# Bias of seven opening M units through TensorE, an earlier third table and later weight loads in a spectral layer with an ELU feed-forward, Trainium2

## The chip, the core and the metric

The kernel runs on one core of a Trainium2 chip. The metric is the time of one execution on the device in microseconds (us). Five engines work side by side, each through its own queue in order: TensorE (PE, matmuls; PEld its weight loads), VectorE (DVE), ScalarE (ACT), GpSimd (POOL) and SyncE (SP), which here only issues transfers. POOL issues transfers too. Matmul results lie in PSUM, everything else in SBUF; DA, DB, inputs and output lie in device memory.

## The reference

Eight sequences of 3008 tokens with 256 features go through a complex linear layer in the frequency domain, a soft threshold, the way back, and then a feed-forward layer with an ELU:

```python
X = np.fft.rfft(x, axis=1)
Yr = Xr @ w_r - Xi @ w_i + b_r
Yi = Xr @ w_i + Xi @ w_r + b_i
Yr = np.sign(Yr) * np.maximum(np.abs(Yr) - lam, 0.0)      # lam = 0.01, Yi alike
y = np.fft.irfft(Yr + 1j * Yi, n=x.shape[1], axis=1)
...
h = y.reshape(8 * 3008, 256) @ w_in                        # 256 x 2048
g = np.where(h > 0.0, h, np.exp(np.minimum(h, 0.0)) - 1.0)
return g @ w_out                                           # 2048 x 256
```

## The kernel before

The transform over 3008 = 47 x 64 points is done in two steps of matmuls each way, with tables M1 to M4 made on the chip in the opening. A sequence passes five kinds of units:

- A (`unit_A`, 6 units): first step, tables M1, from the input tiles `xt`; the result goes to DA in memory and comes back turned as Z (`load_Z`).
- X (`unit_X`, 8 units): second step, table M2, from Z; gives XT. Units with even number make the first half of the features, those with odd number the second. A unit needs one quarter of Z.
- M (`unit_M`, 12 units, numbered (q, i) with q from 0 to 5 and i 0 or 1): the linear layer with `wcat_r` and `wcat_s`, four matmuls of 128x512, the bias, and the soft threshold; gives half of Y(q).
- B (`unit_B`, 6 units): first step back, table M3, from Y(q); the result goes to DB in memory and comes back turned as four parts Bs (`load_Bs`).
- Y (`unit_Y`, 8 units): last step, table M4, from Bs; two units to each part; gives the transposed rows yT of a quarter of the tokens.

The feed-forward then takes blocks of 512 tokens. Each block has eight slots: `front` makes the hidden values of two groups of 128 (`hps`, four matmuls with `w_in_s`), ScalarE and VectorE make the ELU (`Et`, `gT`), and two slots later `back` multiplies by `w_out_r` (eight matmuls). One sequence takes 47 slots. While slots of sequence b run, the units of b+1 and b+2 are put between them, one at the head of a slot, by `plan(b)` (L780): in order Y(2) to Y(5) of the sequence itself, the X units of the next, its M and B units, and the A units of the one after. At b = 0 this list starts in the second slot (slot 1). Y(6) and Y(7) are inserted at places 20 and 24 of the list. The list `f1` holds what is issued in a slot behind `front`: loads and gates.

Everything ahead of the first slot is the opening, written out by hand under a manual schedule: order in the code is order on each engine. It makes the tables, takes sequence 0 through A, X, M and B, sequence 1 through A, and ends with Y(0) and Y(1). The names that matter:

- `idle_pe(n)` (L289): n matmuls of ones that nothing reads.
- `m_group` (L184): the four matmuls of an M unit into PSUM and VectorE's add of `bias_bc`, the bias copied to all 128 partitions, giving `yb` in SBUF (three buffers).
- `first_M(q, i, eng)` (L214): an M unit of the opening with a PSUM tile of its own, from a pool of three (`pre1`). With `nc.gpsimd` POOL clips and subtracts, with `nc.vector` VectorE does. With `nc.scalar` ScalarE makes `clip = relu(yb - lam)`, and VectorE the rest, `min(yb + lam, clip)`, which `let_go` (L209) issues behind the matmuls and the add of the following M unit.
- The third table M3: v3, then w3 = v3 minus its rounded value (L589, L590) and a3 = |w3| (L592), two sines on ScalarE (L595), and two products on VectorE (L601, L607).
- `load_w_in(q)` (L559): a quarter of w_in, 0.5 MB, issued by SP. `scale_w_in(q, ...)` (L638) turns it into a quarter of `w_in_s`.
- `load_w_out(hh)` (L567): half of w_out, 1 MB, issued by POOL.
- `gate(src)` (L571): a one-column copy on POOL, which holds back all of POOL's queue behind it until `src` is there.

The opening's queue of POOL at the X units is: gate on Z, three loads of x for sequence 1, two halves of w_out, and then the clips and subtractions of the M units. SP's queue has the stores of DB, with a quarter of w_in behind each of the first three, then Bs(0), Bs(1), the DA stores of sequence 1 with Bs(2) and Bs(3) between, and the two loads of its Z. A transfer on SP starts in its turn only.

Of the kernel before, what the change touches and what calls it, by code (L numbers as in the profile page):

```python
# [8 lines left out]
ALU = mybir.AluOpType  # L9
AF = mybir.ActivationFunctionType  # L10
# [19 lines left out]
def kernel(  # L30
# [34 lines left out]
    bias_bc = constp.tile([P, 2 * D], F32, name="bias_bc")  # L65
    lam_n = constp.tile([P, 1], F32, name="lam_n")
# [117 lines left out]
    def m_group(b, q, i, ps):  # L184
        XT = XT_of[b]
        o = (2 * q + i) * P
        for m, (c, wm) in enumerate(((0, wcat_r), (1, wcat_s))):
            for dt in range(2):
                nc.tensor.matmul(  # L189
                    ps, lhsT=XT[:, dt, c, o : o + P], rhs=wm[:, dt, :],  # L190
                    start=(m == 0 and dt == 0), stop=(m == 1 and dt == 1),
                )
        if i == 0:
            Y_of[b, q] = wk3.tile([P, 2, 2 * D], BF16, name="Y", tag="Y")
        yb = wk3.tile([P, 2 * D], F32, name="yb", tag="yb")
        nc.vector.tensor_tensor(yb[:], ps, bias_bc[:], ALU.add)  # L196
        clip = wk2.tile([P, 2 * D], F32, name="clip", tag="clip")
        return yb, clip

    def unit_M(b, q, i):  # L200
        if i == 0:
            mps_of[b, q] = unit_ps("mps", False)
        yb, clip = m_group(b, q, i, mps_of[b, q][:, i, :])
        nc.gpsimd.tensor_scalar(clip[:], yb[:], LAM, -LAM, ALU.min, ALU.max)  # L204
        nc.gpsimd.tensor_tensor(Y_of[b, q][:, i, :], yb[:], clip[:], ALU.subtract)  # L205
# [3 lines left out]
    def let_go():  # L209
        for Y_, yb, clip in held:  # L210
            nc.vector.scalar_tensor_tensor(Y_, yb[:], LAM, clip[:], ALU.add, ALU.min)
        held.clear()

    def first_M(q, i, eng):  # L214

        ps = pre1.tile([P, 2 * D], F32, name="mps1", tag="mps1")
        yb, clip = m_group(0, q, i, ps[:])
        let_go()
        Y_ = Y_of[0, q][:, i, :]
        if eng is nc.scalar:  # L220
            nc.scalar.activation(clip[:], yb[:], AF.Relu, bias=lam_n[:])
            held.append((Y_, yb, clip))
        else:
            eng.tensor_scalar(clip[:], yb[:], LAM, -LAM, ALU.min, ALU.max)
            eng.tensor_tensor(Y_, yb[:], clip[:], ALU.subtract)
# [351 lines left out]
    def fB(v, on_dve=False):  # L577
        unit_B(0, v, alone=True, on_dve=on_dve)
# [3 lines left out]
    for ci in range(3):  # L582
        load_x(1, ci)
    load_w_out(0)
    load_w_out(1)
    for u in range(8):
        unit_X(0, u, alone=True, on_dve=u in (1, 4, 7))
        if u == 1:
            nc.vector.tensor_scalar(w3[:], v3[:], CMAGIC, -CMAGIC, ALU.add, ALU.add)  # L589
            nc.vector.tensor_tensor(w3[:], v3[:], w3[:], ALU.subtract)  # L590
        if u == 5:
            nc.scalar.activation(a3[:], w3[:], AF.Abs)  # L592
        idle_pe(1)
# [5 lines left out]
    first_M(0, 0, nc.gpsimd)  # L599
    first_M(0, 1, nc.scalar)  # L600
# [9 lines left out]
    first_M(1, 1, nc.scalar)  # L610
    first_M(2, 0, nc.gpsimd)
    fB(0)
    load_w_in(1)
    first_M(2, 1, nc.scalar)
    first_M(3, 0, nc.gpsimd)
    fB(1)
    load_w_in(2)
    first_M(3, 1, nc.scalar)
    first_M(4, 0, nc.gpsimd)
    fB(2)  # L620
    load_w_in(3)
    first_M(4, 1, nc.scalar)
    first_M(5, 0, nc.scalar)
    fB(3)
    first_M(5, 1, nc.vector)
    idle_pe(3)
    fB(4)
    idle_pe(3)
    fB(5, True)
    M4v = M4[:].rearrange("p (a h) -> p a h", h=2)  # L630
# [7 lines left out]
    def scale_w_in(q, on_dve):  # L638
        dst = w_in_s[:, :, q * FQ : q * FQ + FQ]
        if on_dve:  # L640
            nc.vector.tensor_scalar_mul(dst, w_in_f[q][:], 2.0 / S)
        else:
            nc.scalar.activation(dst, w_in_f[q][:], AF.Copy, scale=2.0 / S)


    scale_w_in(0, True)
    for u in range(6):
        unit_A(1, u, on_dve=bool(u % 2), ahead=True)
        if u in (1, 3):
# [130 lines left out]
    def plan(b):  # L780
# [32 lines left out]
        if b == 0:  # L813
            f1[xs[0]].append((lambda: gate(Z_of[1][:, 16, 0:1]), ()))
# [62 lines left out]
```

## Time and profile before

| | |
|---|---|
| median of 3 runs | 919.3 us (918.46 to 919.53) |
| profiled execution | 918.57 us, span of its profile 916.8 us |
| PE busy | 889.7 us (97%) |
| DVE, ACT, POOL busy | 714.2, 695.8, 314.6 us |
| granted clock of TensorE, mean | 0.997 |
| PE busy, 0 to 100 us | 87.97 us |
| PE busy, 100 to 200 and 400 to 500 us | 97.98 and 99.17 us |
| first Y unit starts | 57.00 us |
| PE idle, 55 to 65 us | 3.03 us |

Busy time is that of instructions that run; idle time of an engine that nobody waits for costs nothing. The chain of waits goes back from the last instruction, at each step to what released it. The windows give, for each stretch of time, how long each engine was busy in it, the clock granted to TensorE (1.00 is full) and the share of the 16 DMA engines.

### The profile page before, as it was taken

The numbers are of one execution on the slowest core, as the hardware profiler recorded it, in microseconds if no ns is written. First come the engines' busy times: TensorE is split into PE (matmuls) and PEld (weight loads), VectorE is DVE, ScalarE is ACT, GpSimd is POOL, SyncE is SP. The second block draws the span as 40 slices with busy tenths as digits, with TensorE's granted clock in tenths as the row PEclk, the third lists the DMA queues.
The fourth block names the chain that finished last, engine by engine and source line by source line (L and its number), as shares of the span: only waits on it lengthen the run. The fifth ranks groups of instructions, "written<-read, shape, count | busy, mean of one in ns | idle before, by whom it ended". The sixth has DMA issues, their size and how long they took to land.

```text
span 916.8 us, 17043 instructions
## 1 busy us (share of the span) xinstructions
PE 889.7 (97%) x6607; PEld 651.7 (71%) x6711; DVE 714.2 (78%) x799; ACT 695.8 (76%) x848; POOL 314.6 (34%) x437
## 2 busy tenths in 40 slices
PE   8889999999999999999999999999999999999997
PEld 3447667776678766886678766787667866777775
DVE  8778778787788778787787877888777877777765
ACT  6667787778777778787787788778887877776664
POOL 6701440333321341405404153033332134343664
PEclk9999999999999999999999999999999999999999
DMA  8984216621284214632266032852228111331011
GB/s 264 357 252 149 92 48 184 207 69 48 70 236 132 70 47 139 188 112 74 65 194 198 24 96 61 216 159 73 66 78 222 29 42 47 88 79 42 26 46 46
DMA packets 90657, 106.23 MB, mean 116 GB/s; under 512 B 5264, under 2 KB 81296, under 8 KB 87216
## 3 DMA queue, kind: packets, MB, share of 16 engines
q1 hardware_dynamic: 84320, 77.61, 30.3%
q0 software_dynamic: 5968, 27.26, 9.2%
q8 instruction: 52, 0.85, 0.4%
q10 hardware_dynamic: 288, 0.26, 0.1%
q14 instruction: 29, 0.24, 0.1%
HBM read 55.31 MB, written 49.81 MB: 115 GB/s over the span
## 4 chain that ended last, share of the span: by engine, by line
PE 79%; DVE 7%; DMA 5%; ACT 5%; issue 3%; POOL 1%; SPq 0%; DVEq 0%; ACTq 0%; POOLq 0%
PE hps L695 31%; PE ps_o L753 31%; PE mps L189 9%; DVE gT L722 2%; PE bps L238 2%; PE yps L276 2%; DVE Et L734 2%; DMA Z<-DA 2%; PE aps L143 2%; ACT Et L709 2%; PE xps L174 2%; DMA Bs<-DB 2%; DMA DA<-A 1%; ACT Et L706 1%; DVE gT L720 1%
## 5 line engine op out<-in xcount | busy, mean ns | idle before, releaser
L753 PE MATMUL ps_o<-w_out_r,gT 128*128 128x256 f32 x3008 | 476.2, 301 | 0.8 <-DVE gT L720 0.8
L753 PEld LDWEIGHTS ps_o<-w_out_r,gT 128*128 128x128 f32 x3008 | 402.4, 189 | 50.1 <-ACT osb L764 1.9
L695 PE MATMUL hps<-yT,w_in_s 128*128 128x512 bf16 (+7 forms) x1653 | 382.3, 351 | 8.7 <-DVE gT L722 1.8
L720 DVE SCALAR_TENSOR_TENSOR gT<-Et,hps 128x1024 fp32r<-128x1024 f32 (+1 forms) x179 | 216.8, 1212 | 88.3 <-POOL Et L732 48.3
L722 DVE SCALAR_TENSOR_TENSOR gT<-hps,Et 128x1024 fp32r<-128x1024 f32 x198 | 242.0, 1222 | 16.0 <-PE hps L695 0.5
L695 PEld LDWEIGHTS <-w_in_s 128*128 128x128 bf16 x1728 | 144.1, 98 | 135.1 <-issue 23.8
L709 ACT ACTIVATE Et<-hps 128x1024 f32<-128x1024 f32 x198 | 204.0, 1031 | 13.5 <-PE hps L695 7.7
L732 POOL TENSOR_SCALAR Et<-Et 128x512 f32<-128x512 f32 x187 | 111.6, 616 | 225.7 <-ACT Et L704 225.7
L734 DVE TENSOR_SCALAR Et<-Et 128x1024 f32<-128x1024 f32 x198 | 136.9, 691 | 45.9 <-ACT Et L709 39.0
L204 POOL TENSOR_SCALAR clip<-yb 128x512 f32<-128x512 f32 x84 | 51.7, 616 | 321.2 <-DVE yb L196 277.9
L704 ACT ACTIVATE Et<-hps 128x512 f32<-128x512 f32 x188 | 102.2, 596 | 67.3 <-PE hps L695 64.5
L706 ACT ACTIVATE Et<-hps 128x1024 f32<-128x1024 f32 x84 | 86.3, 1027 | 72.5 <-PE hps L695 71.0
L205 POOL TENSOR_TENSOR Y<-yb,clip 128x512 bf16<-128x512 f32 x84 | 107.1, 1275 | 7.0
L196 DVE TENSOR_TENSOR yb<-mps,bias_bc 128x512 f32<-128x512 f32 x96 | 66.0, 688 | 36.8 <-PE mps L189 24.1
L707 ACT ACTIVATE Et<-Et 128x1024 f32<-128x1024 f32 x84 | 88.8, 1058 | 2.7
L126 ACT CAST XT<-xps 128x768 bf16<-128x768 f32 x61 | 48.7, 800 | 16.4 <-PE xps L174 16.4
L126 ACT CAST yT<-yps 128x752 bf16<-128x752 f32 x63 | 49.7, 789 | 12.9 <-PE yps L276 12.8
L126 ACT CAST A<-aps 128x1024 bf16<-128x1024 f32 x45 | 45.5, 1014 | 15.8 <-PE aps L143 14.2
L189 PE MATMUL mps<-wcat_r,XT 128*128 128x512 bf16 x177 | 55.4, 388 | 1.0 <-ACT XT L126 0.6
L189 PE MATMUL mps<-wcat_s,XT 128*128 128x512 bf16 x181 | 55.4, 383 | 0.8
L189 PEld LDWEIGHTS <-XT 128*128 128x128 bf16 x384 | 30.7, 98 | 30.7 <-issue 2.5
L251 ACT CAST Bz<-bps 128x1024 bf16<-128x1024 f32 x46 | 46.0, 1000 | 3.0 <-PE bps L238 3.0
(102 smaller groups left out, 404.1 us busy)
## 6 DMA issues: line engine op xcount, KB each, us to landing
xt<-in_x_dram POOLq DMA_DIRECT2D x21, 1024.0 KB, 6.8
out_dram<-osb SPq DMA_DIRECT2D x158, 128.0 KB
Bs<-DB SPq DMA_DIRECT2D x32, 384.0 KB
DA<-A SPq DMA_DIRECT2D x21, 512.0 KB
DB<-Bz SPq DMA_DIRECT2D x21, 512.0 KB
Z<-DA SPq DMA_DIRECT2D x7, 1152.0 KB
Z<-DA SPq DMA_DIRECT2D x11, 384.0 KB
xt<-in_x_dram POOLq DMA_DIRECT2D x6, 512.0 KB, 5.7
```

The costliest lines, as they stand in the source:

```text
L126: nc.scalar.copy(dst, src)
L189: nc.tensor.matmul(ps, lhsT=XT[:, dt, c, o : o + P], rhs=wm[:, dt, :], start=(m == 0 and dt == 0), stop=(m == 1 and dt == 1),)
L205: nc.gpsimd.tensor_tensor(Y_of[b, q][:, i, :], yb[:], clip[:], ALU.subtract)
L695: nc.tensor.matmul(hps[:, s, c0:c1], lhsT=w_in_s[:, dt, ft * P : ft * P + P], rhs=yT_of[b][:, dt, t0 : t0 + c1 - c0], start=(dt == 0), sto ...
L704: nc.scalar.activation(E_[:, s], hps[:, s], AF.Exp)
L706: nc.scalar.activation(E_, hps[:], AF.Relu, scale=-1.0)
L709: nc.scalar.activation(E_, hps[:], AF.Exp)
L720: nc.vector.scalar_tensor_tensor(o, e, -1.0, h, ALU.add, ALU.max)
L722: nc.vector.scalar_tensor_tensor(o, h, 0.0, e, ALU.max, ALU.add)
L732: eng.tensor_scalar(E_[:, s], E_[:, s], 1.0, 0.0, ALU.min, ALU.max)
L734: nc.vector.tensor_scalar(E_, E_, 1.0, -1.0, ALU.min, ALU.add)
L753: nc.tensor.matmul(po[q][:, i_ % 2, :], lhsT=gT[:, s, i_ * P : i_ * P + P], rhs=w_out_r[:, ft, :], start=(ft == 0 and i_ % 2 == 0), stop=( ...
```

## The change

Biased M units. A new bf16 tile `bias_p` holds the bias as three rows, in partitions 0, 32 and 64, and zeros elsewhere; the rows are the bias rounded to bf16, the rest rounded, and the rest of that. A matmul of ones with this tile adds the bias to all rows of a PSUM tile. Seven of the twelve opening M units, those with ScalarE's clip, now start with this matmul, have no add on VectorE, and are read by ScalarE and VectorE from PSUM directly: (0,1), (1,1), (2,1), (3,1), (4,1), (5,0) and (5,1). Before, (5,1) was on VectorE alone. Their PSUM tile is in use until VectorE has made Y.

The rows are loaded six times 256 values on SP at the very beginning into a cleared tile `brow`, and made by six POOL instructions behind the loads of x for sequence 1. The tiles `brow` and `rest` are two of the three `yb` buffers.

M3. w3 is made ahead of the X units and a3 behind the second of them; the products are issued ahead of the adds of M(0,0) and M(1,0). The sine of M4 and the load of the exponential come behind M(1,0).

Weights. w_out's first half is loaded behind the bias rows; its second half behind a gate on Bs(2). w_in's third quarter is loaded behind the last DB store, its fourth behind Bs(3). The third quarter is scaled by ScalarE behind the A units, the fourth by VectorE in two halves in slots 3 and 4 of the loop. Bs(2) and Bs(3) are both issued behind the second A unit. Three idle matmuls ahead of B(4) are gone.

First period. At b = 0, Y(6) and Y(7) come at places 4 and 5 of the list, right behind Y(5), so the units from X(0) on come two slots later, those past the old place 20 one slot later, and those past the old place 24 where they were.

```diff
-    def m_group(b, q, i, ps):
+    def m_group(b, q, i, ps, biased=False):
...
+        if biased:
+            nc.tensor.matmul(ps, lhsT=busy[:, 0:P], rhs=bias_p[:], start=True, stop=False)
...
-        yb = wk3.tile([P, 2 * D], F32, name="yb", tag="yb")
-        nc.vector.tensor_tensor(yb[:], ps, bias_bc[:], ALU.add)
+        if biased:
+            yb = ps
+        else:
+            yb = wk3.tile([P, 2 * D], F32, name="yb", tag="yb")[:]
+            nc.vector.tensor_tensor(yb, ps, bias_bc[:], ALU.add)
...
+    brow, rest = (wk3.tile([P, 2 * D], F32, name="yb", tag="yb") for _ in range(2))
+    nc.vector.memset(brow[:], 0.0)
+    for o, bv in ((0, b_r), (D, b_i)):
+        for k in range(3):
+            nc.sync.dma_start(
+                brow[32 * k : 32 * k + 1, o : o + D],
+                bass.AP(tensor=bv.tensor, offset=bv.offset, ap=[[0, 1], [1, D]]),
+            )
...
     for ci in range(3):
         load_x(1, ci)
+    nc.gpsimd.tensor_copy(bias_p[:], brow[:])
+    nc.gpsimd.tensor_tensor(rest[:], brow[:], bias_p[:], ALU.subtract)
+    nc.gpsimd.tensor_copy(bias_p[32:64], rest[32:64])
+    nc.gpsimd.tensor_copy(bias_p[64:P], rest[64:P])
+    nc.gpsimd.tensor_tensor(rest[64:P], rest[64:P], bias_p[64:P], ALU.subtract)
+    nc.gpsimd.tensor_copy(bias_p[64:P], rest[64:P])
     load_w_out(0)
-    load_w_out(1)
+    nc.vector.tensor_scalar(w3[:], v3[:], CMAGIC, -CMAGIC, ALU.add, ALU.add)
+    nc.vector.tensor_tensor(w3[:], v3[:], w3[:], ALU.subtract)
     for u in range(8):
         unit_X(0, u, alone=True, on_dve=u in (1, 4, 7))
         if u == 1:
-            nc.vector.tensor_scalar(w3[:], v3[:], CMAGIC, -CMAGIC, ALU.add, ALU.add)
-            nc.vector.tensor_tensor(w3[:], v3[:], w3[:], ALU.subtract)
-        if u == 5:
             nc.scalar.activation(a3[:], w3[:], AF.Abs)
...
-    first_M(0, 0, nc.gpsimd)
-    first_M(0, 1, nc.scalar)
     nc.vector.scalar_tensor_tensor(
         M3[:, :, 1, 0:N2], M3[:, :, 0, N2:P], 2.0, sgb, ALU.mult, ALU.mult
     )
...
+    first_M(0, 0, False)
     nc.vector.scalar_tensor_tensor(
         M3[:, :, 1, N2:P], M3[:, :, 0, 0:N2], -2.0, sgb, ALU.mult, ALU.mult
     )
-    first_M(1, 1, nc.scalar)
-    first_M(2, 0, nc.gpsimd)
+    first_M(0, 1, True)
+    first_M(1, 0, False)
+    nc.scalar.activation(r4[:], v4[:], AF.Sin, bias=0.0, scale=TURN)
+    nc.scalar.activation(dume[:], busy[:, 0:1], AF.Exp, scale=0.0)
+    first_M(1, 1, True)
+    first_M(2, 0, False)
     fB(0)
     load_w_in(1)
...
-    first_M(5, 0, nc.scalar)
+    first_M(4, 1, True)
+    first_M(5, 0, True)
     fB(3)
-    first_M(5, 1, nc.vector)
-    idle_pe(3)
+    first_M(5, 1, True)
+    let_go()
     fB(4)
     idle_pe(3)
     fB(5, True)
+    load_w_in(2)
...
     for u in range(6):
         unit_A(1, u, on_dve=bool(u % 2), ahead=True)
-        if u in (1, 3):
-            scale_w_in((u + 1) // 2, True)
-            load_Bs(0, 2 + u // 2)
+        if u == 1:
+            scale_w_in(1, True)
+            for w in (2, 3):
+                load_Bs(0, w)
+            gate(Bs_of[0, 2][:, 0, 0:1])
+            load_w_out(1)
+            load_w_in(3)
         idle_pe(2)
-    scale_w_in(3, False)
+    scale_w_in(2, False)
...
-            seq.insert(20, ("y", 6))
-            seq.insert(24, ("y", 7))
+            seq.insert(20 if b else 4, ("y", 6))
+            seq.insert(24 if b else 5, ("y", 7))
...
         if b == 0:
+            f1[3].append((scale_w_in, (3, True, 0)))
+            f1[4].append((scale_w_in, (3, True, 1)))
             f1[xs[0]].append((lambda: gate(Z_of[1][:, 16, 0:1]), ()))
```

In `first_M` the last argument is now only whether ScalarE clips, and `scale_w_in` has got an argument that names one of the two halves of the contraction.

More of the change, by code (lines that the diff above doesn't have):

```diff
@@ L65 @@
     bias_bc = constp.tile([P, 2 * D], F32, name="bias_bc")
+    bias_p = constp.tile([P, 2 * D], BF16, name="bias_p")
     lam_n = constp.tile([P, 1], F32, name="lam_n")
@@ L190, in m_group @@
                     ps, lhsT=XT[:, dt, c, o : o + P], rhs=wm[:, dt, :],
-                    start=(m == 0 and dt == 0), stop=(m == 1 and dt == 1),
+                    start=(not biased and m == 0 and dt == 0), stop=(m == 1 and dt == 1),
                 )
@@ L203, in unit_M @@
         yb, clip = m_group(b, q, i, mps_of[b, q][:, i, :])
-        nc.gpsimd.tensor_scalar(clip[:], yb[:], LAM, -LAM, ALU.min, ALU.max)
-        nc.gpsimd.tensor_tensor(Y_of[b, q][:, i, :], yb[:], clip[:], ALU.subtract)
+        nc.gpsimd.tensor_scalar(clip[:], yb, LAM, -LAM, ALU.min, ALU.max)
+        nc.gpsimd.tensor_tensor(Y_of[b, q][:, i, :], yb, clip[:], ALU.subtract)
     held = []
@@ L210, in let_go, with first_M @@
         for Y_, yb, clip in held:
-            nc.vector.scalar_tensor_tensor(Y_, yb[:], LAM, clip[:], ALU.add, ALU.min)
+            nc.vector.scalar_tensor_tensor(Y_, yb, LAM, clip[:], ALU.add, ALU.min)
         held.clear()
-    def first_M(q, i, eng):
+    def first_M(q, i, on_act):
         ps = pre1.tile([P, 2 * D], F32, name="mps1", tag="mps1")
-        yb, clip = m_group(0, q, i, ps[:])
+        yb, clip = m_group(0, q, i, ps[:], on_act)
         let_go()
         Y_ = Y_of[0, q][:, i, :]
-        if eng is nc.scalar:
-            nc.scalar.activation(clip[:], yb[:], AF.Relu, bias=lam_n[:])
+        if on_act:
+            nc.scalar.activation(clip[:], yb, AF.Relu, bias=lam_n[:])
             held.append((Y_, yb, clip))
         else:
-            eng.tensor_scalar(clip[:], yb[:], LAM, -LAM, ALU.min, ALU.max)
-            eng.tensor_tensor(Y_, yb[:], clip[:], ALU.subtract)
+            nc.gpsimd.tensor_scalar(clip[:], yb, LAM, -LAM, ALU.min, ALU.max)
+            nc.gpsimd.tensor_tensor(Y_, yb, clip[:], ALU.subtract)
     def unit_B(b, v, alone=False, on_dve=False):
@@ L603 @@
     )
-    nc.scalar.activation(r4[:], v4[:], AF.Sin, bias=0.0, scale=TURN)
-    nc.scalar.activation(dume[:], busy[:, 0:1], AF.Exp, scale=0.0)
-    first_M(1, 0, nc.gpsimd)
+    first_M(0, 0, False)
     nc.vector.scalar_tensor_tensor(
@@ L609 @@
     )
-    first_M(1, 1, nc.scalar)
-    first_M(2, 0, nc.gpsimd)
+    first_M(0, 1, True)
[4 more added lines that the diff above has]
+    first_M(2, 0, False)
     fB(0)
     load_w_in(1)
-    first_M(2, 1, nc.scalar)
-    first_M(3, 0, nc.gpsimd)
+    first_M(2, 1, True)
+    first_M(3, 0, False)
     fB(1)
-    load_w_in(2)
-    first_M(3, 1, nc.scalar)
-    first_M(4, 0, nc.gpsimd)
+    first_M(3, 1, True)
+    first_M(4, 0, False)
     fB(2)
-    load_w_in(3)
-    first_M(4, 1, nc.scalar)
-    first_M(5, 0, nc.scalar)
+    first_M(4, 1, True)
+    first_M(5, 0, True)
     fB(3)
-    first_M(5, 1, nc.vector)
-    idle_pe(3)
+    first_M(5, 1, True)
+    let_go()
     fB(4)
@@ L636, with scale_w_in @@
     load_Bs(0, 1)
-    def scale_w_in(q, on_dve):
-        dst = w_in_s[:, :, q * FQ : q * FQ + FQ]
+    def scale_w_in(q, on_dve, c=slice(0, 2)):
+        dst = w_in_s[:, c, q * FQ : q * FQ + FQ]
         if on_dve:
-            nc.vector.tensor_scalar_mul(dst, w_in_f[q][:], 2.0 / S)
+            nc.vector.tensor_scalar_mul(dst, w_in_f[q][:, c], 2.0 / S)
         else:
-            nc.scalar.activation(dst, w_in_f[q][:], AF.Copy, scale=2.0 / S)
+            nc.scalar.activation(dst, w_in_f[q][:, c], AF.Copy, scale=2.0 / S)
     scale_w_in(0, True)
```

## The prediction

> **What bounds the kernel now.** I read the shares first (PE 97% busy over the span), then the time by stage: before 60 us PE is held up again and again, later only by tenths of a microsecond (of 100 to 800 us it is busy 98 to 99%). All that the change touches lies in the first 80 us, and the steady loop keeps its work. So the question is by how much the start of the loop moves, and whether a new wait appears in the first period. The chain of waits, in order of time (start us, us, what):
>
> ```profile
> 32.26 0.86 DVE M L601
> ...
> 34.80 1.29 DVE M L607
> 36.09 0.05 issue
> 36.13 0.50 PE bps L238 x6
> ...
> 50.59 2.27 DMA DB<-A
> ...
> 52.94 4.02 DMA Bs<-DB
> ...
> 65.16 8.86 DMA Z<-DA
> 74.02 0.05 issue
> 74.07 0.52 PE xps L174 x8
> ```
>
> See that the first B unit waits for the two M3 products on VectorE (34.80 to 36.09), that after the last B unit a store and a load follow at once, so that whatever ends B(5) earlier starts the loop earlier by as much, and that the third X unit of sequence 1 hangs on Z. The timeline round the M units (start us, us, engine, line):
>
> ```profile
> 25.30 1.90 POOL L115 DMA_DIRECT2D xt<-in_x_dram  x3 [0.36 <-PE xps L174]
> ...
> 26.98 2.00 POOL L569 DMA_DIRECT2D w_out_r<-in_moe_w_out_dram  x2
> ...
> 28.83 0.96 DVE L124 CAST XT<-xps 128x768 bf16<-128x768 f32 x1 [1.15 <-PE xps L174]
> ...
> 32.17 0.95 DVE L601 SCALAR_TENSOR_TENSOR M<-M,sg 128x768 bf16<-128x768 bf16 x1
> 32.17 2.08 POOL L225 TENSOR_TENSOR Y<-yb,clip 128x512 bf16<-128x512 f32 x1
> ```
>
> POOL has no work between 13.08 and 19.28 us, but is busy where the change puts the bias rows. L225 took 2.08 us beside L601, where the same form takes 1.27 us later on. And the clock, in half microseconds (PE, PEld, DVE, ACT, POOL busy; granted clock; DMA share; GB/s):
>
> ```profile
> 35.00:35.50 0.50, 0.00 (x0) 0.00 (x0) 0.50 (x1) 0.00 (x0) 0.42 (x2) 1.00 1.00 393
> ...
> 37.50:38.00 0.50, 0.50 (x2) 0.15 (x1) 0.47 (x1) 0.50 (x1) 0.22 (x1) 0.50 1.77 352
> ...
> 40.00:40.50 0.50, 0.50 (x7) 0.09 (x4) 0.50 (x2) 0.00 (x0) 0.11 (x2) 0.50 1.90 344
> ```
>
> After the idle time of PE (34.6 to 36.1) the granted clock is 0.50 from 37.2 to 40.6 us. M(2,1), M(3,0) and B(1) took 3.9 us (36.63 to 40.52) instead of 8 x 0.216 + 0.54 = 2.27, so 1.6 us went there.
>
> **The change part by part.** *Bias row loads.* One memset (like L286, 0.48 us) ahead of VectorE's first columns, and six 1 KB loads on SP (0.36 to 0.66 us of issue each by L154 and L513, some 3 us in all). M1 is ready at 3.91, the first A matmul starts at 5.66, and VectorE waits 1.64 us for ScalarE at 12.9: the memset is hidden, and costs 0.5 if that cover went. SP's first store goes out at 7.83, so the loads are hidden too. I take 0, between 0 and 0.5.
>
> *Third table earlier.* w3 (L589 0.55, L590 0.96) goes into the 1.93 us that VectorE waits ahead of 24.08; Abs (L592, 0.85) goes behind the first X evacuation on ScalarE, 24.32 to 25.17, where the next is due at 25.20. So ScalarE's last X evacuation and the two sines come 0.45 us sooner, but the first M group still waits for VectorE's X evacuation to end at 29.79. The first M unit stays at 29.84 to 30.70. Cost 0, M3 products possible from 29.9.
>
> *The bf16 rows.* POOL runs four casts and two subtractions behind the x loads, from 27.2 (25.30 + 1.90). Casts at 0.61 (L507) and subtractions at 1.27 (L205, L225) give 4 x 0.61 + 2 x 1.27 = 4.98, so 32.2. If the casts of 32 and 64 partitions ran beside one another, 0.6 less: 31.6. If M3's products shut POOL out as L601 did L225 (2.08 - 1.27 = 0.8), 0.8 for one and 2.0 for all that can collide (twice 0.8, and 0.3 for the last cast as L224's 0.92 against 0.62): 33.0 or 34.2. One collision is likeliest, since the first product becomes possible in the midst of the chain: 33.0. [...]
>
> *What waits for it.* M(0,1), second in PE's queue, could start at 30.70 and now waits until 33.0; all later M units are queued behind it. Its five matmuls take 5 x 0.216 = 1.08 (to 34.1), M(1,0) 0.86 (35.0), M(1,1) 1.08 (36.0). M(2,0) needs M(0,1)'s PSUM buffer back: ScalarE's clip 0.6 (L704's 128x512 from PSUM, 596 ns), VectorE's add for M(1,0) 0.69 from 35.0, then Y(0,1) 0.69, so 36.4. It ends at 37.2, and B(0) at 37.8 (0.54). POOL is not later: w_out's one issue 1.1 from 33.0, clip 0.62 and Y 1.27, so 36.0, or 36.8 with a collision. Before, B(0) ended at 36.63: 1.2 us are lost here.
>
> *What it buys.* VectorE drops seven of twelve adds and the clip and subtraction of M(5,1) (0.42, 0.69), and three idle matmuls (0.65) go ahead of B(4). PE pays 7 x 0.216 = 1.5 us for the bias. From B(0): two rounds of 1.08 + 0.86 + 0.54 = 2.48 reach 42.8; M(4,1), M(5,0), B(3) take 2.70, 45.5; M(5,1) and B(4) 1.62, 47.1. The last half of B(5) waits for M(5,1)'s end at 46.6 + 0.6 + 0.69 + hand-overs 0.1 = 48.0 and ends at 48.3, against 49.23: 0.9 us gained if the clock stays up. PE stands still for 2.3 us at M(0,1), longer than the 1.54 that brought the half clock before, so I expect it again. It costs 0 to 1.6; as part falls on the wait for M(2,0)'s buffer, I take 0.6. Net gain at B(5): 0.3. [...]
>
> *Weights later.* w_in(2) is issued (0.51) behind the last DB store, which Bs waits 2.27 for anyway: 0, at most 0.3 if its 0.5 MB delays Bs. w_out(1) (issue 1.1) stands on POOL behind Bs(2)'s landing, where POOL is idle until 74.08, and w_in(3) on SP ahead of two DA stores and both Z loads. The DMA engines were full from 57 to 64 us, at 336 GB/s on average by the windows, so 1.5 MB more put the last DA landing back by 4.6 us. Y(6) and Y(7) now come ahead of the X units, so the third X unit is due at 78.0 (73.7 + two slots of 2.15) instead of 73.7; Z would be there at 74.02 + 4.6 = 78.6. The wait of 0.35 becomes 0.6; 0 if w_out fits into the gap at 64 to 66 us (36 and 66 GB/s), 1.6 if issues back up too. I take 0.2, a gain of 0.15. Bs(3) goes out one A pair earlier and is needed 9 slots on: 0. The last w_in quarter is scaled by two halves on VectorE in slots 3 and 4 (0.68 / 2 = 0.34 each), where hps comes free only 0.16 to 0.24 us before PE wants it: 0 to 0.5, I take 0.2. It lands near 65 (0.9 MB left at 59.5, at half of 336 GB/s, 5.4 us), VectorE wants it at 67.2.
>
> **The sum.** -0.3 (opening) - 0.15 (Z) + 0.2 (scaling) = -0.25. The profiled execution took 918.57 (span 916.8 and 1.8 around it), 0.7 under the median of the runs, 919.3. Against the median I forecast 919.0: no change.
>
> **Rivals.** *1. The rows are ready early, and the opening shortens (faster).* The casts overlap and M3's products don't collide: 31.6. M(0,1) waits 0.9, less than the 1.54 that slowed the clock; B(0) ends 1.4 sooner than in the forecast's 37.8 and so does B(5), 46.9 against 49.23: -2.3. The third X unit then finds Z ready, -0.35, scaling +0.1: -2.6, 916.7. For it: no row shows these casts on few partitions. Against: L225.
>
> *2. The rows become the bound (slower).* POOL is shut out every time, rows at 34.2, B(0) 1.2 later than in the forecast, and the 3.5 us of idle PE bring the half clock in full, 1.6 instead of 0.6. B(5) is then at 48.9 + 1.2 + 1.0 = 51.1, +1.9; with scaling 0.2, +2.1: 921.4. It decides once the rows come after 33.4. For it: L224 takes 0.92 instead of 0.62 in this stretch, L225 1.86 and 2.08. Against: only two products can collide.
>
> *3. The weights in front of Z (slower).* If SP also stands at a full queue, as for 2.12 us at Bs(3)'s issue (L265), Z lands at 80.7 for an X unit due at 78.0: 2.7 - 0.35 = 2.3 on top of the forecast's -0.1 without the Z term: +2.2, 921.5.
>
> *4. VectorE wasn't what held up the M units*, so seven fewer adds buy nothing: then rival 2 or the forecast; L607 and the half clock cost more than any add.
>
> **Chances.** A measurement tells this kernel from no change at about 0.2%, 1.8 us. Forecast 0.42, rival 1 0.29, rival 2 with 4 0.20, rival 3 0.09. So faster 0.29, same 0.42, slower 0.29. The range reaches from just under rival 1 to just past rivals 2 and 3, 916.2 to 921.8. The forecast's own is 917.5 to 920.8.
>
> **What would show it.** The start of the bias matmul of M(0,1) (33.0, rivals 31.6 and 34.2), the spans of the six POOL instructions, the granted clock in the 3.4 us behind it, the end of B(5) (48.9), the start of the first Y unit (57.0 before), and what ends PE's idle time before the third X unit. I am wrong if PE doesn't stand at M(0,1), or if the loop starts as forecast and the end doesn't follow it.

## The result and the profile after

The changed kernel takes 921.84 us (median of 8 runs, 919.99 to 923.36) against 919.23 of the kernel before in the same job (917.44 to 919.62): ratio 1.0031, 95% interval 1.0018 to 1.0043. It is slower by some 2.6 us, just past the upper end of the range. The profiled execution took 921.08, span 919.3.

From the start of the first Y to the end of the span both kernels take the same: 859.8 before (916.8 - 57.0), 859.6 after (919.3 - 59.66). So, in sum, all of the loss lies ahead of 60 us. (Behind the first Y the changed kernel first falls back a little: its eighth group of `hps` starts 17.98 after the first Y, 17.42 before the change. Some 360 us after the first Y it has made this up.) GpSimd's timeline of the changed kernel (start us, us, engine, line, [idle before]):

```profile
27.20 0.85 POOL L598 CAST bias_p<-yb 128x512 bf16<-128x512 f32 x1
28.12 1.16 POOL L599 TENSOR_TENSOR yb<-yb,bias_p 128x512 f32<-128x512 f32 x1
29.35 0.60 POOL L600 CAST bias_p<-yb 32x512 bf16<-32x512 f32 x1
30.00 0.61 POOL L601 CAST bias_p<-yb 64x512 bf16<-64x512 f32 x1
30.68 1.97 POOL L602 TENSOR_TENSOR yb<-yb,bias_p 64x512 f32<-64x512 f32 x1
32.72 1.22 POOL L603 CAST bias_p<-yb 64x512 bf16<-64x512 f32 x1
```

VectorE's two products of the third table stand beside the last two of them:

```profile
30.68 0.96 DVE L617 SCALAR_TENSOR_TENSOR M<-M,sg 128x768 bf16<-128x768 bf16 x1
31.67 0.69 DVE L202 TENSOR_TENSOR yb<-mps,bias_bc 128x512 f32<-128x512 f32 x1
32.28 1.19 DVE L621 SCALAR_TENSOR_TENSOR M<-M,sg 128x768 bf16<-128x768 bf16 x1
```

The subtraction L602 starts with L617 and takes 1.97 instead of the 1.16 of L599; the cast L603 runs into L621 and takes 1.22 instead of 0.61. The chain lasts 6.74 from 27.20 and the rows are ready at 33.94. TensorE's timeline shows who waits, and the half-microsecond windows (PE, PEld, DVE, ACT, POOL busy; granted clock; DMA share; GB/s) what follows:

```profile
33.99 0.38 PE L189 MATMUL mps<-bias_p,busy 128*128 128x512 bf16 x1 [2.36 <-POOL bias_p L603]
...
59.66 0.51 PE L282 MATMUL yps<-M,Bs 96*128 96x94 bf16 x8 [1.00 <-DMA Bs<-DB]
```
```profile
33.00:33.50 0.50, 0.00 (x0) 0.00 (x0) 0.47 (x1) 0.00 (x0) 0.50 (x1) 1.00 1.09 426
36.00:36.50 0.50, 0.50 (x2) 0.15 (x1) 0.00 (x0) 0.48 (x2) 0.50 (x1) 0.50 0.69 139
38.00:38.50 0.50, 0.50 (x3) 0.22 (x2) 0.23 (x1) 0.00 (x0) 0.42 (x2) 0.50 1.44 352
40.00:40.50 0.50, 0.50 (x8) 0.18 (x3) 0.50 (x2) 0.19 (x1) 0.00 (x0) 1.00 0.24 59
```

TensorE stands 2.36 for the rows, and the granted clock is 0.50 from 35.2 to 38.6 behind it. B(0) ends at 40.27 (before 36.63), B(5)'s matmuls at 51.34 (before 49.22), and the chain of waits then has the store and the load that it had before (2.27 and 4.02):

```profile
52.72 2.63 DMA DB<-A
55.54 4.08 DMA Bs<-DB
```

In the loop the wait of 0.35 for Z at the third X unit is gone, but there is a new one:

```profile
67.74 1.23 DVE L742 SCALAR_TENSOR_TENSOR gT<-hps,Et 128x1024 fp32r<-128x1024 f32 x1 [1.44 <-PE ps_o L773]
```
```profile
69.01 1.02 PE L715 MATMUL hps<-yT,w_in_s 128*128 128x512 bf16 x4 [0.96 <-DVE gT L742]
```

The second gT is written only when the first `back` (L773) has read the first gT. In the built program both have one SBUF address; before the change the second gT took the buffer of the A tile that leaves first. The A tiles of sequence 1 come from the same three buffers (L133 of the changed kernel), and which of them the pool hands out next depends on the order of the work around; two other orders, e4 and e10 below, give the second gT the A tile's buffer again, in e4 without a wait.

### The profile page after: what moved, and what is told of

Same layout as the page of the kernel before. It is cut to its first block, busy times and chain, and to the rows that moved or that the text cites. A ratio compares the mean times of both kernels' runs of the same rounds, so it can differ in the third digit from the quotient of the medians.

```text
span 919.3 us, 17070 instructions
## 1 busy us (share of the span) xinstructions
PE 890.7 (97%) x6611; PEld 652.8 (71%) x6715; DVE 709.8 (77%) x793; ACT 696.7 (76%) x849; POOL 319.4 (35%) x444
## 4 chain that ended last, share of the span: by engine, by line
PE 80%; DVE 6%; ACT 4%; DMA 4%; issue 3%; POOL 2%; SPq 0%; DVEq 0%; ACTq 0%; POOLq 0%
PE hps L715 32%; PE ps_o L773 32%; PE mps L192 9%; DVE gT L742 3%; PE bps L244 2%; PE yps L282 2%; DVE Et L754 2%; ACT Et L729 2%; PE aps L144 2%; PE xps L175 2%; DMA Bs<-DB 2%; DVE gT L740 1%; DVE osb L784 1%; DMA Z<-DA 1%; DMA xt<-in_x_dram 1%
## 5 line engine op out<-in xcount | busy, mean ns | idle before, releaser
L773 PE MATMUL ps_o<-w_out_r,gT 128*128 128x256 f32 x3008 | 476.0, 301 | 0.9 <-DVE gT L740 0.9
L773 PEld LDWEIGHTS ps_o<-w_out_r,gT 128*128 128x128 f32 x3008 | 402.2, 189 | 50.1 <-ACT osb L784 1.9
L715 PEld LDWEIGHTS <-w_in_s 128*128 128x128 bf16 x1728 | 144.1, 98 | 135.9 <-issue 24.9
L202 DVE TENSOR_TENSOR yb<-mps,bias_bc 128x512 f32<-128x512 f32 x89 | 61.3, 689 | 40.5 <-PE mps L192 23.1
```

Source lines behind the costliest of these rows:

```text
L715: nc.tensor.matmul(hps[:, s, c0:c1], lhsT=w_in_s[:, dt, ft * P : ft * P + P], rhs=yT_of[b][:, dt, t0 : t0 + c1 - c0], start=(dt == 0), sto ...
L773: nc.tensor.matmul(po[q][:, i_ % 2, :], lhsT=gT[:, s, i_ * P : i_ * P + P], rhs=w_out_r[:, ft, :], start=(ft == 0 and i_ % 2 == 0), stop=( ...
```

## The experiments

Three theories: (1) the rows come late and the clock behind that wait doubles the price; (2) the moved loads cost by themselves; (3) gT's buffer costs 0.96. Their rival: the opening is bounded by something else, so that mending one moves the wait. The table has all runs. "Bias" is the start of the first biased matmul, B(5) the end of its matmuls, loop the span less the first Y, all from the profiled execution; the ratio is to the kernel before in the same job. The profiled execution of e14 was late from the start (below), so its first three columns don't compare.

| run | bias | B(5) | first Y | loop | ratio, 95% interval |
|---|---|---|---|---|---|
| kernel before | - | 49.22 | 57.00 | 859.8 | 1 |
| changed kernel | 33.99 | 51.34 | 59.66 | 859.6 | 1.0031 (1.0018, 1.0043) |
| e1 rows early | 35.28 | 50.94 | 59.61 | 859.9 | 1.0046 (1.0034, 1.0059) |
| e2 busy wait | 33.71 | 49.37 | 57.75 | 859.9 | 1.0023 (1.0013, 1.0034) |
| e3 two rows | 30.80 | 46.46 | 54.98 | 860.2 | 0.9988 (0.9979, 0.9997) |
| e4 loads back | 33.87 | 50.84 | 58.76 | 859.5 | 1.0026 (1.0016, 1.0037) |
| e5 table alone | - | 46.51 | 56.06 | 860.5 | 0.9999 (0.9990, 1.0007) |
| e6 two rows, loads back | 30.12 | 45.79 | 56.58 | 860.4 | 1.0008 (0.9999, 1.0017) |
| e7 rows before x | 30.41 | 46.94 | 55.43 | 860.1 | 0.9996 (0.9987, 1.0004) |
| e8 the same, loads back | 30.25 | 47.65 | 60.45 | 860.8 | 1.0053 (1.0040, 1.0066) |
| e9 four gT | 34.34 | 51.69 | 60.76 | 860.3 | 1.0031 (1.0020, 1.0043) |
| e10 w_in(2) behind Bs | 33.51 | 50.86 | 58.75 | 863.4 | 1.0052 (1.0037, 1.0067) |
| e11 e7 and e10 | 31.80 | 47.46 | 55.08 | 863.1 | 1.0013 (1.0004, 1.0021) |
| e12 e11, loads spread | 31.45 | 48.50 | 58.79 | 863.1 | 1.0046 (1.0034, 1.0058) |
| e13 fill before Y | 33.95 | 51.30 | 59.75 | 861.7 | 1.0047 (1.0034, 1.0060) |
| e14 both fills, four gT | 36.14 | 51.81 | 60.29 | 859.9 | 1.0015 (1.0006, 1.0024) |
| e15 e7, fill, four gT | 30.38 | 46.50 | 55.28 | 864.0 | 0.9995 (0.9987, 1.0004) |
| e16 before, fill | - | 48.33 | 56.20 | 859.3 | 1.0005 (0.9996, 1.0015) |
| e17 two rows, four gT | 30.12 | 45.78 | 54.60 | 859.4 | 0.9979 (0.9970, 0.9988) |
| e18 e7, four gT | 30.42 | 46.68 | 55.25 | 860.9 | 0.9989 (0.9981, 0.9998) |

### The late rows (e1, e2, e3)

e1: the six GpSimd instructions ahead of the copies of `wcat`, which stand before the x loads.

```diff
         pool.tensor_tensor(v4[:], v4[:], r4[:], ALU.subtract)
+        nc.gpsimd.tensor_copy(bias_p[:], brow[:])
+        ...
```

> The six POOL instructions that make the bias rows stand ahead of the copies of wcat, where POOL waited from 13.1 to 19.3 us before. Late rows (my theory): rows ready near 19, M(0,1) follows M(0,0) with no gap, no wait of 2.4 us and no half clock behind it, B(5) ends near 47 instead of 51.3, first Y unit near 55.3 instead of 59.7, time 4 to 4.5 us under the changed kernel's 921.8, so about 917.5, under the kernel before. Rival, VectorE shut out: the chain falls among VectorE's two-input work for M2, X starts up to 1.5 us later, 919. Rival, the weight loads are the cause: rows early change nothing, 921 to 922.

The six ended at 19.77 and the first biased matmul did not wait; still the kernel got no faster. TensorE's timeline of e1:

```profile
25.00 0.50 PE L175 MATMUL xps<-M,Z 96*128 96x96 bf16 x8 [3.58 <-DVE M L487]
```

The first X unit waits for the second table on VectorE until 25.0 (before 22.97), with the half clock through the X units after it (from 26.66 on eight matmuls take 0.80 to 0.84, the first two eights 0.50). What the rows gave was taken away in front of them, since VectorE's instructions for that table grew beside the six. One of them, of the same form, in the changed kernel and in e1:

```profile
16.25 0.35 DVE L443 TENSOR_SCALAR st<-kv 96x384 f32<-96x384 f32 x1
```
```profile
18.10 1.20 DVE L443 TENSOR_SCALAR st<-kv 96x384 f32<-96x384 f32 x1
```

Early GpSimd work beside VectorE's tables is no place for the rows either.

e2: eleven matmuls of ones ahead of M(0,1), so that TensorE stays busy through the wait.

```diff
+    idle_pe(11)
     first_M(0, 1, True)
```

> Eleven idle matmuls (2.4 us) fill PE's wait ahead of M(0,1); the rows come as late as in the changed kernel, 33.9. If the wait also costs by the half clock behind it: granted clock 1.00 from 34 to 40 us, B(5) 1.0 to 1.6 us sooner, about 920.5. If the half clock has another cause or costs nothing on the path: 921.8.

The rows are as late, but the granted clock stays at 1.00 in every window from 30 to 70, and B(5) ends 1.97 earlier (51.34 to 49.37), of which 0.28 is the rows (33.99 to 33.71). The rest, 1.7, is the clock's share of the loss in this execution. By the medians it is less: they moved from 1.0031 to 1.0023 of the kernel before, some 0.7 us, with overlapping intervals.

e3: the third bias row is left out.

```diff
-        for k in range(3):
+        for k in range(2):
...
-    nc.gpsimd.tensor_copy(bias_p[64:P], rest[64:P])
-    nc.gpsimd.tensor_tensor(rest[64:P], rest[64:P], bias_p[64:P], ALU.subtract)
-    nc.gpsimd.tensor_copy(bias_p[64:P], rest[64:P])
```

> Leaves out the third row (the bias is added with two bf16 rows), and with it three of the six POOL instructions and two of the six loads. Late rows: rows ready near 30.0, M(0,1) waits for nothing, B(0) near 36.4, B(5) near 47, about 917.5. If POOL's lateness isn't what counts: 921.8.

```profile
30.80 0.38 PE L189 MATMUL mps<-bias_p,busy 128*128 128x512 bf16 x1
...
54.98 0.84 PE L282 MATMUL yps<-M,Bs 96*128 96x94 bf16 x16 [1.19 <-DMA Bs<-DB]
```

In e3's timeline the bias matmul has no idle time in brackets: nobody waits, B(5) ends 4.9 sooner than in the changed kernel and 2.8 sooner than before. Theory 1 holds. But of the 2.8 only 2.0 reach the first Y, 1.6 the profiled times (916.98 against 918.57), and 0.85 the medians (917.04 against 917.89).

### The moved loads (e4, and e5 to e8)

e4: bias and table as changed, the loads, the scaling and Y(6), Y(7) as before.

```diff
     load_w_out(0)
+    load_w_out(1)
...
     fB(1)
+    load_w_in(2)
...
     fB(2)
+    load_w_in(3)
```

> All weight loads, Bs loads, scalings and Y(6), Y(7) stand where they were before; bias rows and third table as changed. Late rows: PE still waits for the rows until about 34; only the half microsecond between the end of B(5) and the first Y unit comes back (8.3 us in the changed kernel, 7.8 before), and the 0.35 us wait for Z is there again: 921.3 to 921.8. If the moved loads are the cause: 919.2, as before.

B(5) to first Y is 7.92 instead of 8.32 and gT's wait is gone; the ratio is below the changed kernel's, but its interval overlaps (1.0016 to 1.0037 and 1.0018 to 1.0043). I read this as "the moved loads are a loss of their own", and the next runs showed that reading to be wrong. e5 is the kernel before with the third table alone made early:

```diff
+    nc.vector.tensor_scalar(w3[:], v3[:], CMAGIC, -CMAGIC, ALU.add, ALU.add)
+    nc.vector.tensor_tensor(w3[:], v3[:], w3[:], ALU.subtract)
     for u in range(8):
...
+    nc.vector.scalar_tensor_tensor(
+        M3[:, :, 1, 0:N2], M3[:, :, 0, N2:P], 2.0, sgb, ALU.mult, ALU.mult
+    )
     first_M(0, 0, nc.gpsimd)
```

> The kernel before with the third table alone made early (its two arguments ahead of the X units, its products ahead of the additions of M(0,0) and M(0,1)); the bias stays on VectorE, the loads stay where they were. Theory A (in the changed kernel the early table is worth what lay before B(0) in the kernel before: the wait of 1.5 for the last product of the table, with the half clock behind it): no wait for the product, B(0) ends by 35.2 instead of 36.6, B(5) at 47.0 to 48.0 instead of 49.2, the median 1.2 to 2.2 below the kernel before. Theory B (VectorE's additions are what sets the rounds of M and B, so the table alone only moves the wait to the next addition): B(5) at 48.7 to 49.5, the median within 0.6 of the kernel before.

e6 is e3 with e4's edit:

> The changed kernel without the third bias row (its two loads and three GpSimd instructions are left out, so the bias is rounded to two bf16 rows) and with the loads, the scaling and the late Y units where they were before. Theory A (late rows and moved loads are two losses that add): rows ready at 30 to 31, first Y at 54.2 to 54.9, no wait of gT for the matmuls of the first pair, the median 2.2 to 3.2 below the kernel before, 1.3 to 2.2 below the run with two rows and moved loads (0.9988 of the kernel before). Theory B (the moved loads cost nothing by themselves and what the first batch showed of them was the clock behind the wait): the same as the run with two rows, 0.4 to 1.3 below the kernel before.

e7 has three rows, the six instructions ahead of the x loads; e8 is e7 with e4's edit:

```diff
     gate(Z_of[0][:, 8, 0:1])
+    nc.gpsimd.tensor_copy(bias_p[:], brow[:])
+    ...
     for ci in range(3):
         load_x(1, ci)
```

> The changed kernel with all three rows, the six GpSimd instructions put ahead of the three x loads on the same queue (behind the gate on Z). Theory A (the rows are late only because the three issues stand ahead of the six instructions; VectorE's part of the opening is not shut out at that place as it was when the six stood among the early table work): rows ready by 30.5, the first biased matmul waits less than 0.3, B(5) at 46.3 to 47.5 with no half clock behind M(0,0), the median 0 to 1.5 below the kernel before. Theory B (the six instructions lengthen each other and VectorE's work wherever they stand, as in the run that moved them among the table work): rows ready by 30.5 too, but X units late by 1 to 3, B(5) at 48.5 to 51, the median 1 to 4 above the kernel before.

> The kernel of the run before this one with the loads, the scaling and the late Y units back where they were. Theory A (two separate losses): first Y at 54.2 to 55.2, the median 1.3 to 3.0 below the kernel before and 0.9 to 2.0 below the run with the moved loads. Theory B (early x loads and early weights share the transfer engines with the table stage and delay Z's or XT's work once the rows no longer hold them back): X units later by 0.5 or more and the median within 1.0 of the run with the moved loads.

e7 came out as its theory A has it: the bias matmul waits for nobody, B(5) ends at 46.94, and the median is 0.5 below the kernel before. Its second subtraction and last cast, ahead of the table's products, show what the collision cost in the changed kernel (1.97 and 1.22 there):

```profile
28.44 1.15 POOL L600 TENSOR_TENSOR yb<-yb,bias_p 64x512 f32<-64x512 f32 x1
29.65 0.61 POOL L601 CAST bias_p<-yb 64x512 bf16<-64x512 f32 x1
```

e5's first half came out better than either theory said: B(5) ends 2.7 sooner, with the bias still on VectorE. Yet the time is the same, 0.9999. With the loads in their old places an earlier B(5) finds Bs late. TensorE's first Y in the kernel before, in e5, e6 and e8:

```profile
57.00 0.84 PE L276 MATMUL yps<-M,Bs 96*128 96x94 bf16 x16 [0.46 <-DMA Bs<-DB]
```
```profile
56.06 0.84 PE L276 MATMUL yps<-M,Bs 96*128 96x94 bf16 x16 [2.23 <-DMA Bs<-DB]
```
```profile
56.58 1.43 PE L282 MATMUL yps<-M,Bs 96*128 96x94 bf16 x16 [3.48 <-DMA Bs<-DB]
```
```profile
60.45 1.44 PE L282 MATMUL yps<-M,Bs 96*128 96x94 bf16 x16 [5.47 <-DMA Bs<-DB]
```

The windows of e5 say why and what it brings:

```profile
44.00:48.00 4.00, 2.99 (x20) 1.03 (x16) 2.86 (x6) 3.19 (x5) 0.50 (x2) 1.00 1.09 379
...
58.00:60.00 2.00, 2.00 (x9) 0.90 (x10) 0.00 (x0) 0.14 (x1) 0.00 (x0) 0.50 1.08 338
```

The DMA engines are full (share 1.09 at 379 GB/s; it adds up the times of the packets, and reached 1.86 in the kernel before from 38 to 40) until 48 with x, w_out and w_in, so the last DB stores queue: from the issue of the last two stores to that of the first Bs load e5 takes 6.28 (45.85 to 52.13), the kernel before 4.36 (48.58 to 52.94), e8 9.19 (47.40 to 56.59). e8 against e7, in the windows from 48 to 52 us:

```profile
48.00:52.00 4.00, 3.70 (x17) 1.54 (x15) 3.25 (x5) 2.30 (x3) 0.00 (x0) 1.00 1.16 370
```
```profile
48.00:52.00 4.00, 3.71 (x16) 1.81 (x16) 3.54 (x5) 1.66 (x2) 0.00 (x0) 1.00 0.82 230
```

The first is e8, full at 370 GB/s where B(5)'s stores want to go; the second is e7. Behind the waits of 2.23 and 3.48 the clock is halved again (0.50 at 58 to 60 in e5 and in e6). So theory A of e6 and e8, two losses that add, falls, and theory B of neither has the size: with the rows in time, putting the loads back costs 5.0 at the first Y (e7 to e8) and 1.6 (e3 to e6). In the kernel before, matmul chain and transfers were nearly level; the early table pays only with the late loads. What the late loads are worth by themselves, in the kernel before, was not run.

### gT's buffer and w_in(2) (e9 to e12)

```diff
-            gT = late3.tile([P, 2, TB], F32R, name="gT", tag="gT")
+            gT = late3.tile([P, 2, TB], F32R, name="gT", tag="gT", bufs=4)
```

> The changed kernel with a fourth buffer for gT and the A tiles beside it, so that the second gT takes a buffer that nobody holds. Theory A (the 0.96 that TensorE stands at the fourth matmul group of the loop is the second gT waiting until the first has been read): that idle is under 0.1 and the span from first Y to the end is 0.7 to 1.1 shorter (858.5 to 858.9 instead of 859.6), all before first Y as in the changed kernel; the median 1.2 to 2.4 above the kernel before (the changed kernel: 2.6 above). Theory B (VectorE is late there by itself, with the scaling of the fourth quarter of w_in in front): the idle stays at 0.8 to 1.0 and the loop at 859.4 to 859.9.

The idle of 0.96 is gone, so it was the buffer (theory A of e9), but the loop did not get shorter in this execution: a wait of 1.74 for Bs stood ahead of the first Y, and the half clock behind it fell on the loop (62.1 to 65.5; four `hps` matmuls at 62.63 took 1.89 instead of 1.02).

e10 sends w_in(2) behind the first two Bs loads; e11 does that to e7.

```diff
     fB(5, True)
-    load_w_in(2)
...
     load_Bs(0, 1)
+    load_w_in(2)
```

> The changed kernel with the third quarter of w_in sent behind the first two Bs loads instead of ahead of them; in the built program the second gT then gets the buffer of an A tile, as in the kernel before. Theory A (that quarter in front of Bs is what lengthened the way from B(5) to first Y, and gT's buffer is the idle in the loop): B(5) to first Y 7.7 to 8.0 instead of 8.3, no idle of 0.96 in the loop, the median 0.9 to 1.8 above the kernel before. Theory B (the way to first Y is long because of the transfers behind DB, whichever goes first): B(5) to first Y stays at 8.2 to 8.6; only the idle goes, the median 1.4 to 2.4 above.

> The changed kernel with both: the six GpSimd instructions ahead of the x loads, and the third quarter of w_in behind the first two Bs loads. Theory A (gains add, since the moved loads keep the transfers out of the way of DB and Bs): first Y at 54.8 to 55.3, no idle of 0.96 in the loop, the median 1.0 to 2.0 below the kernel before. Theory B (the transfers bound the way to first Y as in the kernels with the loads back): first Y not before 55.4, the median 0.4 to 1.2 below.

B(5) to first Y fell to 7.89 and 7.62, as theory A said, so w_in(2) ahead of Bs does cost 0.4. But neither theory had what comes next, in e10's ScalarE and TensorE:

```profile
61.33 1.06 ACT L660 ACTIVATE w_in_s<-w_in_f 128x1024 bf16<-128x1024 f32 x1 [4.33 <-DMA w_in_f<-in_moe_w_in_dram]
62.30 0.77 ACT L127 CAST yT<-yps 128x752 bf16<-128x752 f32 x1
```
```profile
63.12 1.86 PE L715 MATMUL hps<-yT,w_in_s 128*128 128x512 bf16 x4 [3.52 <-ACT yT L127]
```

The scaling of w_in(2) stands ahead of the first yT in ScalarE's queue, waits 4.33 for its data, and TensorE loses 3.5. With ScalarE's work in this order, w_in(2) is better sent ahead of Bs, as in the change. Nor did the A tile's buffer help e10: its second gT waited for that tile's store to DA, and TensorE stood 0.83 there instead of 0.96. e12, which spread the four loads of GpSimd's queue between its M units, shares this loss, and its later x and w_out fell on the DB stores (332 GB/s from 48 to 52 us, e11 135; wait for Bs 2.96):

> The kernel of the run before this one, with the three x loads and the first half of w_out spread between GpSimd's M work: one x load ahead of M(0,0), one behind it, one behind M(1,0), w_out behind M(2,0). Theory A (M(0,0)'s two GpSimd instructions, and B(0) behind them, wait for four DMA issues that end at 33.0): M(0,0)'s first instruction by 31.2, B(0) starts by 34.2 instead of 35.1, first Y 0.6 to 1.2 earlier, the median 1.6 to 3.0 below the kernel before. Theory B (GpSimd has no room for an issue in a round of M and B, 0.63 beside 1.9 of work in 2.58, or the later transfers fall on DB's stores): B units at 2.7 or more a round, first Y within 0.4 of the run before, the same time.

### What is left, and a version that beats both (e13 to e18)

e13 has eight instead of three filler matmuls ahead of the first Y, e16 six in the kernel before, e14 fills both waits and has four gT, e15 is e7 with filler and four gT.

> The changed kernel with eight instead of three filler matmuls ahead of the first Y, so that TensorE is busy through the wait of 1.0 to 1.7 for Bs. Theory A (in part of the executions that wait halves the clock at the first Y, which is why the changed kernel's times spread over 3.4): first Y within 0.3 of 59.7, no half clock behind it, times within 2.2 of each other, the median 1.0 to 2.2 above the kernel before (the changed kernel: 2.6). Theory B (the spread comes from the wait for the bias rows alone): spread and median as in the changed kernel, 2.3 to 3.2 above.

> The changed kernel with eleven filler matmuls ahead of M(0,1), eight instead of three ahead of the first Y, and a fourth buffer for gT: what is left of its losses is the late rows themselves. Theory A (late rows, the clock behind two waits, and gT's buffer are the whole loss): first Y at 57.5 to 58.1, no half clock from 24 to 75 but for the X units, no idle of 0.96, the median within 0.7 of the kernel before. Theory B (something else is lost that these do not touch, in the transfers or in the loop): the median 0.8 to 2.0 above the kernel before.

> The changed kernel with the six GpSimd instructions ahead of the x loads, eight instead of three filler matmuls ahead of the first Y, and a fourth buffer for gT. Theory A (each of the three losses goes, and the moved loads keep the transfers clear of DB and Bs): first Y at 55.2 to 55.7, the loop 858.5 to 859.0 from there, the median 1.2 to 2.6 below the kernel before. Theory B (the wait for Bs only grows by what is won ahead of it, or the filler stands in the way): first Y after 55.9 and the median within 0.9 of the kernel before.

> Control: the kernel before with six instead of three filler matmuls ahead of the first Y. Theory A (its wait of 0.46 for Bs rarely halves the clock, and the filler is no gain of its own): the median within 0.6 of the kernel before. Theory B (the filler helps whatever kernel it stands in): 0.8 to 1.6 below, and as much of the gain of the run before this one is the filler's and not the change's.

The filler ahead of Y gains nothing in either kernel (e13, e16). e13, 4.0 above the kernel before, is even worse than its theory B, and its times spread over 3.4 as the changed kernel's do, so that spread has another source. Its profiled execution, close to its median, shows a candidate:

```profile
74.00 1.23 DVE L742 SCALAR_TENSOR_TENSOR gT<-hps,Et 128x1024 fp32r<-128x1024 f32 x1 [2.07 <-DMA DA<-A]
```
```profile
75.28 1.02 PE L715 MATMUL hps<-yT,w_in_s 128*128 128x512 bf16 x4 [1.70 <-DVE gT L742]
```

The fourth gT takes the buffer of the last A tile and waits for that tile's store to DA. In the changed kernel it takes the same buffer and is not held up: it starts at 71.94, half a microsecond after the last packet of the stores (71.47). In how many executions this margin is used up is not shown.

With the clock kept up at both waits and gT freed e14 is still 0.15% slower (theory B's 0.8 to 2.0): the late rows by themselves and what these edits don't touch, which the runs don't part. Its profiled execution is the slowest of its eleven: TensorE waited 1.85 for a part of x at 10.24, and the first X unit started at 25.65 (changed kernel 23.16). e15's median is 1.0 below the kernel before, between its theories; its profiled execution too is the slowest (921.07 against a median of 917.81), and shows what the moved loads leave no room for:

```profile
73.92 0.51 PE L175 MATMUL xps<-M,Z 96*128 96x96 bf16 x8 [1.82 <-DMA Z<-DA]
```

Its Z loads went out at 69.52, 14.2 behind the first Y (kernel before 7.8, e17 10.9). The DMA engines were full with the DA stores, w_out and w_in until 67 (share 1.05, 1.16 and 1.44 in the windows from 60 to 66); by the packets in the trace, the data of the stores was through at 66.6, but the last packet of 4 bytes on their queue ended only at 68.86, together with the last one of w_out. Why it took so long is open. It is the price named as rival 3, in one execution, and e13's wait is the same price in another place.

e17 is e3, e18 is e7, each with four gT and no filler:

> The run with two bias rows (its third row is left out) and a fourth buffer for gT. Theory A (gT's wait of 0.96 is worth its length once the rows are in time): no idle of 0.96, span from first Y to the end 859.0 to 859.5 instead of 860.2, the median 1.4 to 2.6 below the kernel before (the run with two rows alone: 0.9988 of it). Theory B (what gT gives is taken back where TensorE then waits for the Z load, which the moved w_out and w_in hold back, and which already cost 0.5 at the tenth matmul group of the loop): the idle at Z grows to 1.0 or more and the median is within 0.5 of the run with two rows alone, 0.5 to 1.4 below the kernel before.

> Three bias rows with the six GpSimd instructions ahead of the x loads and a fourth buffer for gT, without the filler ahead of the first Y. Theory A (the filler is worth nothing, since in the changed kernel it gained nothing): the median 0.6 to 2.0 below the kernel before, as with the filler or better, the same first Y within 0.4. Theory B (the wait for Bs halves the clock in part of the executions): times over 918.5 in a third or more of them and the median 0 to 0.6 below.

e17, whose bias has two bf16 rows instead of three, is 0.21% faster than the kernel before (916.82 against 919.06); e18, with all three rows, 0.11%, as its theory A has it, though 4 of its 11 times lie over 918.5, as in theory B. Both intervals lie below 1. In e17 the idle at gT is gone and Z's wait with it (theory A). The first X unit of the loop starts 16.65 behind the first Y, against 17.67 in e3. That fourth buffer is worth about 0.08% by the ratios (0.9988 to 0.9979, 0.9996 to 0.9989), whose intervals overlap; in the profiles of the three kernels with three rows and four buffers (e9, e14, e18) most of the 0.96 is lost again later in the loop (between 447 and 513 and between 622 and 665 us behind the first Y), and why is open.

## Why the prediction was wrong

The first Y came 3.0 later than forecast (59.66 against 57.0 - 0.3). By the profiled execution four terms make this up: the rows 1.0 (the bias matmul at 33.99 instead of 33.0), the clock behind the wait for them 1.1 (1.7 instead of 0.6), the rounds up to B(5) 0.4, and the way from B(5) to the first Y 0.5. From there the loop took what was forecast within 0.2, though by other waits.

*The rows.* This is the first step that failed. "One collision is likeliest" gave 33.0. Both products fell on the chain: L602 took 0.8 more than L599, L603 0.6 more than L601. The first cast behind the x issues took 0.85 instead of 0.61, and the gaps between instructions, left out of the sum, made 0.33. Casts on 32 and 64 partitions took 0.60 and 0.61, no less than on 128 (0.61, L507 of the kernel before). 33.94 lies past 33.4, from which rival 2 was said to decide, and near its 34.2.

*The clock.* This is the second: I charged 0.6 of 1.6, and it came in full. From the start of the bias matmul to the end of B(5) the changed kernel, e9, e10 and e13, which have the half clock behind the wait, take 17.35 each; e1, e2, e3, e11 and e17, which have none there, take 15.66. (In e7, e8, e15 and e18 the loads on GpSimd's queue stand ahead of M(0,0)'s clip, B(0) waits for it, and the stretch is 16.1 to 17.4 at full clock.) B(5) then came at 51.34; rival 2 said 51.1, with 921.4 for the time (921.84).

*Seven additions off VectorE.* The rounds took 2.59 instead of 2.48. Once the rows are in time B(5) ends at 46.46 (e3); rival 1 said 46.9. But most of that is not bought by the additions: e5, with all twelve on VectorE, ends B(5) at 46.51. In e5 the X units began 0.7 sooner than in e3 (22.74 against 23.44), so the better pair is e5 and e6: both end B(0) at 34.7, and then e6 ends B(5) 0.72 sooner (45.79). That is what the additions are worth; the early table, with the wait and the half clock that it removes, brings the rest. Rival 4 was right for the larger part.

*"Whatever ends B(5) earlier starts the loop earlier by as much"* was wrong, and no rival had it. This is the step that keeps the gain small even where the rows are in time. e5 won 2.7 at B(5) and 0.9 at the first Y, e6 3.4 and 0.4. The transfers were a second limit just under the first. It can be read before the change: by the windows of the kernel before, the DMA share is 1.04 or more in every 2 us from 30 to 48.

*Weights later.* w_in(2) was priced 0 to 0.3; B(5) to first Y grew by 0.54, and e10 shows 0.43 of it. The Z loads went out 12.35 behind the first Y instead of 7.80, 4.55 later where 4.6 was forecast, and Z's wait went, as said. The scaling on VectorE made no wait that the profile shows; gT's buffer, 0.96, was in no term. The two are terms of a few tenths and of one, and with the rows in time they eat a good part of the gain: e3's B(5) is 2.8 sooner than before, its profiled time 1.6, its median 0.85.

## What to carry to other kernels

Before counting a gain on the critical path, ask what else is nearly full there: two limits that lie level (here the matmul chain and the DMA engines) gave little when one of them was moved (e5: 2.7 at B(5), 0.9 at the first Y). An engine's preparation that landed on a chain with a waiting TensorE was paid twice, 2.36 as the wait and 1.7 as the clock behind it (changed kernel, e2); make it shorter (two rows, e3) or put it where neither VectorE's work nor its own queue holds it back (e7). And a reordered load can change which buffer a tile pool hands out next, so look at the addresses of the first tiles after it.

## What the runs showed of the hardware

- The granted clock changed on a grid of 3.41 us, whose place differs from execution to execution: in the first 88 us of the 20 traces, as far as they record the clock, every stretch at half clock is one, two or three such steps long (37.23 to 40.64 in the kernel before, 57.31 to 64.13 in e5, 58.78 to 69.02 in e12). In these traces, of the full-clock steps in which TensorE was busy for under 48%, all 17 were followed by half clock (11% at 30.91 in e13, 46% at 70.94 in e15); from 49 to 54%, 3 of 9 (49% at 33.81 in the kernel before, but not 49% at 20.16 there); from 55% on, none of 422. The length of a wait alone did not tell it: behind waits of 1.54 (kernel before), 1.74 (e9), 1.82 (e15) and 2.36 (changed kernel) the clock was halved, behind 1.50 (e17) and 1.70 (e13, 1.00 in every window from 74 to 84) it was not. The steps that hold the waits of 2.36 and 1.50 (first the step, its length and PE's busy time):

```profile
31.78:35.20 3.42, 1.21 (x6) 0.58 (x6) 1.69 (x2) 0.00 (x0) 3.28 (x4) 1.00 1.08 429
```
```profile
51.11:54.53 3.42, 1.99 (x8) 0.71 (x7) 1.33 (x2) 1.77 (x2) 0.00 (x0) 1.00 0.93 263
```

- In the changed kernel's profile even the X units at 24.9 to 28.4 ran at 0.50 (eight matmuls in 0.85; TensorE was busy 1.85 of 3.41 in the step ahead of them), in e3's and e18's they did not (0.50 to 0.52).
- VectorE and GpSimd took longer beside each other here: VectorE's L443 took 1.20 instead of 0.35 beside GpSimd's bias rows (e1), GpSimd's subtraction 1.97 beside VectorE's product (changed kernel) instead of 1.15 (e7).
- GpSimd took 0.60 for a cast of 32 partitions, 0.61 for 64 and 0.61 for 128 (L600 and L601 of the changed kernel; e18's first).
- The opening moved by 1.4 us between two executions: behind the same code the first biased matmul started at 30.41 in e7 and 31.80 in e11. In e11 the first X unit waited 2.13 for Z, and eight X matmuls took 0.82 to 0.85 from 25.02 on instead of 0.50.
